# Holding all stores behind the last load, 22 output places and a new instruction order in a fused gated-attention and maxout kernel

## The chip, the cores and the metric

The kernel runs on one core of a Trainium2 chip. The metric is device time in microseconds (us), from launch to end, of that core. The trace's span, from the first to the last traced instruction, is a little shorter. Every number below is from a timed run or from a trace, unless the Trainium skill is named for it. "TensorE" is PE in the profile, "VectorE" DVE, "ScalarE" ACT, "GpSimd" POOL, and "SyncE" SP, the engine that issues nearly all transfers here, in the order of its own instruction stream.

## The reference, cut to what matters

```python
# q, k, v, alpha: (4, 8, 768, 48) float32; out: (3072, 384) float32
for t in range(S):                                  # S = 768
    state = alpha[:, :, t, :, None] * state + einsum('bhd,bhe->bhde', k[:, :, t], v[:, :, t])
    y[:, :, t] = einsum('bhd,bhde->bhe', q[:, :, t], state)
x = y.transpose(0, 2, 1, 3).reshape(B * S, H * D)   # (3072, 384)
g = maximum(x @ w1, x @ w2)                         # w1, w2: (384, 1024)
out = g @ w_out                                     # (1024, 384)
```

Inputs are 4.72 MB each for q, k, v and alpha, weights another 4.72 MB, and 4.72 MB are written.

## The kernel before

The 3072 tokens are cut into 24 chunks of 128. The first six chunks (the first batch) are loaded and computed as three pairs; their tiles carry a d in front (`dcs`, `dqt`, `dpt`, `dy`). The other 18 are single chunks: four loads of 192 KB each, so 72 loads. Per chunk, `loga` is the logarithm of alpha, `cs` its cumulative sum as a matrix product, `ep` and `en` its exponentials, `qt` and `kt` the scaled q and k, `tp` their transposes, `pa`/`pb` the masked scores (`pt`), `T` the carried state, `y` the attention output. Then come the maxout products: `h`, `g`, `op` and the output row block.

The program is ordered while it is built. Each piece of work is an `Op` with its engines, dependencies, buffers and a priority. A list scheduler with a model of durations decides, from a table `PLAN` of nudges, which piece is emitted next on which engine. Each engine then runs its own list strictly in that order, SyncE too. The parts that matter here:

```python
def load(n, i):                     # single chunks: into the old weight staging buffers, six chunks deep
    ...
    nc.sync.dma_start(out=t, in_=src[b, :, c * C : (c + 1) * C, :].rearrange("h p d -> p h d"))

def oevict(e, t0):                  # output rows from PSUM to SBUF; NO = 6 places
    outs[t0] = mo.tile([128, DM], FP32, tag="outs", name="outs", bufs=NO)
    copy(e, outs[t0], ops[t0])

def store(t0):
    nc.sync.dma_start(out=out[t0 : t0 + C, :], in_=outs[t0])
# ... (cut)
op("st", a + i, {"SP": 0.55}, lambda e, t=a0 + i * C: store(t), lat=1.2, deps=[ev], reads=[bs],
   prio=-1, slack=3.0 if a + i < NCG - 4 else 0.0)

def dcs(m, h):                      # cumulative sum of a pair of chunks: 4 wide and 4 narrow products
    l = [loga[:, j, hr(h), 0:D] for j in range(2)]
    nc.tensor.matmul(cs[:, 0:X], lhsT=c11, rhs=l[0], start=True, stop=False)
    nc.tensor.matmul(cs[:, X : 2 * X], lhsT=c11, rhs=l[0], start=False, stop=False)
    nc.tensor.matmul(cs[:, X : 2 * X], lhsT=c11, rhs=l[1], start=False, stop=False)
    nc.tensor.matmul(cs[:, 0:X], lhsT=c01, rhs=l[1], start=False, stop=False)
    # ... four products of 4 columns
```

A store thus stands among the loads. When SyncE reaches one whose output is not ready, the loads behind it wait too.

Of the kernel before, what the change touches and what calls it, by code (L numbers as in the profile page):

```python
# [15 lines left out]
class Op:  # L16


    def __init__(self, sched, name, n, engs, fn, deps=(), lat=0.1, alloc=(), reads=(), prio=0.0, tiled=False, after=(), slack=0.0,
                 shared=False):  # L20
        early, wait, only = PLAN.get(f"{name} {n}", (0.0, 0.0, None))
        engs = {only: engs[only]} if only in engs else engs
        prio, slack = prio + early, slack + wait
        self.name, self.n, self.engs, self.fn, self.lat = name, n, engs, fn, lat
        self.deps, self.alloc, self.prio, self.tiled = [d for d in deps if d is not None], list(alloc), prio, tiled
        self.after = [d for d in after if d is not None]
        self.left, self.done, self.slack, self.shared = None, None, slack, shared
        for b in list(alloc) + list(reads):
            b.users.append(self)
        for e in engs:  # L30
            sched.todo[e].append(self)
# [22 lines left out]
class Banks:  # L54
# [21 lines left out]
COLD = {"m": 2.0, "dp4": 1.3}  # L76
# [4 lines left out]
    "den (2, 1)": (0.0, 0.8, None), "f (0, 4)": (-2.0, 0.0, None), "dm1 (2, 0)": (-1.0, 0.4, None),  # L81
    "dt32 (1, 0)": (0.0, 0.8, None), "m0 21": (0.0, 0.2, None), "v2 15": (0.0, 0.8, None), "qt 19": (-3.7, 0.0, None),
    "oev 12": (0.0, 0.0, 'ACT'), "dv2 (0, 1)": (-1.0, 0.0, None), "w2c (1, 1)": (0.0, 0.4, None),
    "m0 6": (0.0, 0.6, None), "relu (4, 2)": (0.0, 0.4, None), "p3 23": (2.0, 0.0, None), "m 2": (-20.0, 0.0, None),
    "relu (13, 7)": (-4.0, 0.0, None), "ep 18": (20.0, 0.0, None), "mev 2": (4.0, 0.8, None),
    "p2 20": (-900.0, 0.0, None), "mask 0": (21.0, 0.0, None), "den (2, 0)": (-3.0, 0.0, 'DVE'),
    "p3 14": (-900.0, 0.0, None), "T0 19": (0.0, 0.0, 'POOL'), "dp1 (0, 1)": (0.0, 0.2, 'ACT'),
    "dqt (1, 1)": (-0.3, 0.0, None), "w2c (0, 0)": (-0.3, 0.0, 'ACT'), "dm0 (0, 0)": (0.0, 0.8, None),
    "relu (4, 4)": (0.0, 0.4, None), "dp3 (1, 0)": (-1.0, 0.2, None), "f (19, 1)": (900.0, 0.0, None),
    "one 2": (898.0, 0.0, None), "one 0": (-900.0, 0.4, None), "p1 16": (-20.0, 0.0, None),  # L90
    "dep (2, 1)": (0.3, 0.0, None), "en 13": (0.0, 0.8, None), "w 12": (0.0, 0.8, None), "p2 12": (0.0, 0.4, None),
    "dgg (2, 1)": (0.0, 0.4, None), "w 10": (0.0, 0.0, 'DVE'), "dt32 (0, 1)": (-2.3, 0.0, None),
    "t32 14": (0.3, 0.0, 'ACT'), "p2 16": (2.0, 0.0, None), "f (2, 0)": (0.0, 0.2, None),
    "t (5, 1)": (-900.0, 0.2, None), "en 11": (0.0, 0.2, None), "dT1 (0, 1)": (2.0, 0.0, None),
    "dT0 (0, 1)": (1.0, 0.0, None), "f (2, 7)": (-0.3, 0.0, None), "v2 16": (0.0, 0.8, None),
    "dv2 (1, 0)": (0.0, 0.0, 'DVE'), "g 11": (4.0, 0.0, None), "dT0 (1, 0)": (0.0, 0.8, None),
    "relu (7, 0)": (-2.0, 0.0, None), "t (1, 1)": (0.3, 0.0, None), "a1 11": (20.0, 0.4, None),
    "dg (0, 1)": (1.3, 0.0, None), "qt 23": (-899.0, 0.0, None), "oev 6": (0.0, 0.2, None),
    "p3 8": (-900.0, 0.0, None), "T1 7": (6.0, 0.0, None), "one 1": (-1.0, 0.0, None), "f (0, 0)": (-4.0, 0.0, None),
    "dv (1, 0)": (1.0, 0.0, None), "v1 15": (1.0, 0.0, None), "relu (13, 4)": (0.0, 0.0, 'POOL'),  # L100
    "v2 6": (0.0, 0.8, None), "f (13, 0)": (-900.0, 0.0, None), "f (0, 1)": (-2.0, 0.0, None),
    "da3 (0, 0)": (20.3, 0.0, None), "dkt (1, 1)": (0.0, 0.0, 'ACT'), "p2 23": (0.3, 0.0, None),
    "g 17": (0.0, 0.8, None), "dv2 (1, 1)": (0.0, 0.0, 'DVE'), "qt 7": (0.3, 0.0, None),
    "dp1 (2, 1)": (-900.0, 0.0, None), "kt 7": (-0.3, 0.0, None), "dv (2, 1)": (0.0, 0.2, None),
    "m0 11": (900.0, 0.0, None),
# [3 lines left out]
class Sched:  # L109
# [7 lines left out]
    def __init__(self):  # L117
        self.todo = {e: [] for e in ("PE", "ACT", "DVE", "POOL", "SP")}
        self.free = {e: 0.0 for e in self.todo}
        self.wire = 2.0  # L120
        self.tiled = False
        self.refill = None
# [51 lines left out]
    def run(self):  # L174
        while True:
# [14 lines left out]
            if e == "PE" and t < 19.0:  # L190
                cost *= COLD.get(op.name, 1.65)
            if op.shared:

                cost += min(cost, max(0.0, self.free["POOL"] - t) / 2)
            if e == "PE" and op.tiled != self.tiled:
                cost += 0.09
# [21 lines left out]
def kernel(  # L218
# [27 lines left out]
    ND = NCH // 2  # L246
# [8 lines left out]
    ldp = ctx.enter_context(tc.tile_pool(name="ldp", bufs=2))  # L255
# [14 lines left out]
    def load(n, i):  # L270
# [4 lines left out]
        o = (4 * (n % 2) + i) * H * D  # L275
        t = loads[n][i] = flat[:, o : o + H * D].rearrange("p (h d) -> p h d", h=H)
        nc.sync.dma_start(out=t, in_=src[b, :, c * C : (c + 1) * C, :].rearrange("h p d -> p h d"))

    dloads = {m: [None] * 4 for m in range(ND)}

    def dload(m, i, h=None):
        src, tag = SRC[i]
        if dloads[m][i] is None:
            dloads[m][i] = ldp.tile([128, H, 2 * D], FP32, tag="d" + tag, name="d" + tag, bufs=2)
# [3 lines left out]
            in_=src[0, hs, m * C2 : (m + 1) * C2, :].rearrange("h (p j) d -> p h (j d)", j=2),  # L288
# [61 lines left out]
    NB, NQ, NPT = 3, 4, 4  # L350
# [13 lines left out]
    def set_mask():  # L364
        for u in range(2):
            ps = slice(64 * u, 64 * u + 64)
            for jk, jq in ((0, 0), (0, 1), (1, 1)):
                nc.vector.tensor_copy(out=cmask[ps, jk, 64 * jq : 64 * jq + 64], in_=u16[ps, ps])
            nc.vector.tensor_sub(out=cmask[ps, 1, 0:64], in0=u16[ps, ps], in1=ident16[ps, ps])
# [26 lines left out]
    xT = constp.tile([128, 3, NT], FP16)  # L396

# [36 lines left out]
    def v1k(n):  # L434
        nc.gpsimd.tensor_mul(out=kts[n % NB][:, :, 0:D], in0=loads[n][1], in1=st[n]["en"])  # L435

    def v1v(n, t):
        vp = loads[n][3].rearrange("p (r t) d -> p t r d", t=2)
        nc.gpsimd.tensor_copy(out=v16s[n % NB][:, :, 64 * t : 64 * t + D], in_=vp[:, t])
# [5 lines left out]
    def vT(n, t):  # L445
# [4 lines left out]
        nc.gpsimd.tensor_mul(  # L450
# [5 lines left out]
    def vt32(n):  # L456
        t32 = st[n]["t32"] = wk.tile([128, NP, D], FP32, tag="t32", name="t32")
        nc.gpsimd.tensor_mul(  # L458
# [106 lines left out]

    def dcs(m, h):
# [4 lines left out]
        nc.tensor.matmul(cs[:, 0:X], lhsT=c11, rhs=l[0], start=True, stop=False)  # L571
        nc.tensor.matmul(cs[:, X : 2 * X], lhsT=c11, rhs=l[0], start=False, stop=False)
        nc.tensor.matmul(cs[:, X : 2 * X], lhsT=c11, rhs=l[1], start=False, stop=False)
        nc.tensor.matmul(cs[:, 0:X], lhsT=c01, rhs=l[1], start=False, stop=False)
        for r in range(2):
            o = 2 * X + 4 * r
            for j in range(2):
                nc.tensor.matmul(
                    cs[:, o : o + 4], lhsT=loga[:, j, 4 * h + 2 * r : 4 * h + 2 * r + 2, :], rhs=gcol4,
                    start=False, stop=(r == 1 and j == 1),  # L580
                )
# [17 lines left out]
    def dqk(m, h, i):  # L599
# [3 lines left out]
        else:  # L603
            nc.gpsimd.tensor_mul(out=dkts[m % 2][:, :, hr(h), 0:D], in0=src, in1=sd[m]["en"][:, :, hr(h)])  # L604
# [45 lines left out]
    def more(m, u):  # L650
        return u == 0 or m < ND - 1
# [17 lines left out]
    def dw(m, u):  # L669
# [3 lines left out]
        if m == 0 and u == 0:  # L673
# [12 lines left out]
    def dt32(m, u):  # L686
        m1, u1 = dbefore(m, u)
        t32 = sd[m]["t32", u] = wk.tile([128, NP, D], FP32, tag="dt32", name="dt32")
        nc.gpsimd.tensor_mul(out=t32, in0=sd[m1]["w", u1], in1=sd[m]["g", u].unsqueeze(2).to_broadcast([128, NP, D]))

    def dT(m, u, t):
        m1, u1 = dbefore(m, u)
        ps = slice(64 * t, 64 * t + D)
        nc.gpsimd.tensor_mul(
# [4 lines left out]
    def dy(m):  # L699
# [13 lines left out]
        for u in range(2):  # L713
            if u == 1 or m:
# [93 lines left out]
    def ocols(e, t0, c):  # L808
        if c == 0:
            outs[t0] = mo.tile([128, DM], FP32, tag="outs", name="outs", bufs=NO)  # L810
# [7 lines left out]
    outs = {}  # L818

    def oevict(e, t0):  # L820
        outs[t0] = mo.tile([128, DM], FP32, tag="outs", name="outs", bufs=NO)
# [6 lines left out]
    NG, NO = 3, 6  # L828
# [5 lines left out]
    rg16, ro = Ring(NG), Ring(NO)  # L834
# [9 lines left out]
    LOAD, WLOAD = 1.0, 4.12  # L844
# [14 lines left out]
    def dloads_of(m, margin):  # L859
        nonlocal prev  # L860
        dbl.append([Buf(r) for r in rdl])
        parts = [(i, h) for h in (0, 1) for i in (0, 1, 2)] + [(3, None)] if m == 0 else [(i, None) for i in range(4)]
        for i, h in parts:
            prev = op("dld", m, {"SP": DL[m] / (1 if h is None else 2)}, lambda e, i=i, h=h: dload(m, i, h), lat=margin,
                      alloc=[dbl[m][i]] if not h else (), reads=[dbl[m][i]] if h else (), after=[prev], prio=0.3 + m)
# [6 lines left out]
    for x in "d0 w20 w21 wo0 wo1 w10 w11 d1 d2".split():  # L872
        if x[0] == "d":
            dloads_of(int(x[1]), (1.0, 1.9, 1.8)[int(x[1])])
        else:
# [10 lines left out]
           for f in range(0, NF, 2)]  # L886
    for n in range(2 * ND, NCG):
# [28 lines left out]
    smask = op("mask", 0, {"DVE": 1.8}, lambda e: set_mask(), prio=0.1)  # L916
# [7 lines left out]
    for m in range(ND):  # L924
# [18 lines left out]
        for h in range(2):  # L943
# [3 lines left out]
                alloc=al("loga"), reads=[L[0]] + re("loga"))  # L947
            add("p1", h, {"PE": 0.43}, lambda e, m=m, h=h: dcs(m, h), [g["a1", h]], lat=0.17, alloc=[("cs", h)], reads=["loga"])
# [6 lines left out]
            add("kt", h, {"POOL": 0.94}, lambda e, m=m, h=h: dqk(m, h, 1), [g["en", h], g["ld", 1, h]],  # L955
                alloc=al("kt"), reads=["en", L[1]] + re("kt"))
            add("qt", h, {"DVE": 0.47}, lambda e, m=m, h=h: dqk(m, h, 2), [g["ep", h], g["ld", 2, h]], shared=True,
                alloc=al("qt"), reads=["ep", L[2]] + re("qt"))
# [178 lines left out]
```

## Time and profile before

| | before |
|---|---|
| timed runs supplied with the kernel | 147.58 us median of 3 (147.46 to 147.76) |
| time of the profiled run itself, and its span | 144.87 us, 143.1 us |
| TensorE busy | 128.9 us, 90% of the span |
| DMA share, first four fifths of the span | 0.8 to 1.0 in nearly every slice |

The run that was traced took 144.87 us and its span is 143.1 us. The profile lines for this kernel stand in the prediction below.

### The profile page before, as it was taken

The numbers are of one execution on the slowest core, as the hardware profiler recorded it, in microseconds if no ns is written. First come the engines' busy times: TensorE is split into PE (matmuls) and PEld (weight loads), VectorE is DVE, ScalarE is ACT, GpSimd is POOL, SyncE is SP. The second block draws the span as 40 slices with busy tenths as digits, with TensorE's granted clock in tenths as the row PEclk, the third lists the DMA queues.
The fourth block names the chain that finished last, engine by engine and source line by source line (L and its number), as shares of the span: only waits on it lengthen the run. The fifth ranks groups of instructions, "written<-read, shape, count | busy, mean of one in ns | idle before, by whom it ended". The sixth has DMA issues, their size and how long they took to land.

```text
span 143.1 us, 4890 instructions
## 1 busy us (share of the span) xinstructions
PE 128.9 (90%) x1969; PEld 89.4 (62%) x1969; DVE 88.6 (62%) x167; ACT 96.1 (67%) x221; POOL 81.8 (57%) x183
## 2 busy tenths in 40 slices
PE   0377899996999999999999999987999999999991
PEld 0266647774777666766676666645666676666770
DVE  4639739599698985978586858444767856600100
ACT  3552946836876797669785978559659964674541
POOL 6896300499976967776379498407687953400000
PEclk9999999999999999999999999999999999999999
DMA  4999999999989889999899799979998992000403
GB/s 114 250 332 385 379 364 250 233 268 230 202 184 220 175 167 220 236 183 239 200 241 191 175 235 208 184 156 245 225 239 168 223 235 105 35 30 5 165 0 110
DMA packets 93686, 28.62 MB, mean 200 GB/s; under 512 B 87904, under 2 KB 92128, under 8 KB 93664
## 3 DMA queue, kind: packets, MB, share of 16 engines
q1 hardware_dynamic: 93520, 28.22, 83.0%
q8 instruction: 15, 0.25, 0.7%
q10 hardware_dynamic: 144, 0.10, 0.2%
q14 instruction: 7, 0.06, 0.1%
HBM read 23.59 MB, written 4.72 MB: 198 GB/s over the span
## 4 chain that ended last, share of the span: by engine, by line
PE 70%; POOL 10%; DMA 6%; DVE 5%; SPq 3%; issue 2%; ACT 2%; POOLq 0%; ACTq 0%
PE h L777 17%; PE op L794 17%; PE op L791 6%; PE y L548 5%; PE mp L766 4%; DMA wof<-in_alpha_dram 4%; PE pa L489 3%; PE tp L471 3%; DMA daf<-in_alpha_dram 3%; PE dy L710 3%; PE tp L473 2%; POOL kt L435 2%; PE cs L413 2%; PE dtp L616 2%; POOL dkt L604 2%
## 5 line engine op out<-in xcount | busy, mean ns | idle before, releaser
L794 PE MATMUL op<-wo,g 128*128 128x384 f16 x184 | 35.5, 326 | 0.0
L777 PE MATMUL h<-xT,wd 128*128 128x384 f16 (+1 forms) x216 | 34.2, 308 | 0.0
L777 PEld LDWEIGHTS <-wd 128*128 128x128 f16 x216 | 20.3, 98 | 9.0
L794 PEld LDWEIGHTS <-g 128*128 128x128 f16 x184 | 17.2, 98 | 10.7
L784 ACT ACTIVATE g<-h 128x384 f16<-128x384 f32 (+1 forms) x52 | 22.1, 462 | 1.5 <-PE h L777 1.2
L738 ACT COPY qk<-tp 128x1024 f16<-128x1024 f16 x15 | 15.2, 1014 | 4.3 <-PE tp L473 4.2
L508 DVE TENSOR_TENSOR pt<-pa,u 128x512 f16<-128x512 f32 x18 | 11.9, 687 | 9.7 <-PE pa L489 5.4
L782 DVE TENSOR_SCALAR g<-h 128x384 f16<-128x384 f32 (+1 forms) x20 | 9.9, 514 | 12.8 <-PE h L777 12.6
L450 POOL TENSOR_TENSOR T<-w,g 48x192 f16<-48x192 f32 x30 | 15.1, 502 | 1.2
L738 ACT COPY outs<-op 128x384 f32<-128x384 f32 x18 | 8.8, 488 | 9.8 <-PE op L794 9.8
L791 PE MATMUL op<-m,xT 128*128 128x384 f16 x69 | 15.0, 325 | 0.0
L604 POOL TENSOR_TENSOR dkt<-dkf,den 128x384 f16<-128x384 f32 x6 | 6.5, 1085 | 11.7 <-ACT den L586 11.6
L508 DVE TENSOR_TENSOR pt<-pb,u 128x512 f16<-128x512 f32 x18 | 11.8, 680 | 0.0
L519 DVE TENSOR_TENSOR w<-kv,t 48x192 f32<-48x192 f32 x24 | 8.5, 352 | 2.4 <-POOL t L458 1.3
L552 ACT CAST xT<-y 128x384 f16<-128x384 f32 x18 | 8.0, 478 | 2.9 <-PE y L548 2.8
L423 ACT ACTIVATE en<-cs 128x384 f32<-128x384 f32 x18 | 9.0, 497 | 1.1 <-PE cs L417 1.0
L423 ACT ACTIVATE ep<-cs 128x384 f32<-128x384 f32 x18 | 9.0, 499 | 0.0
L435 POOL TENSOR_TENSOR kt<-wof,en 128x384 f16<-128x384 f32 x6 | 6.3, 1056 | 4.2 <-ACT en L423 4.2
L548 PE MATMUL y<-pt,v 128*32 128x128 f16 x288 | 8.2, 219 | 0.0
L791 PEld LDWEIGHTS <-xT 128*128 128x128 f16 x69 | 6.1, 97 | 3.1
L435 POOL TENSOR_TENSOR kt<-w1f,en 128x384 f16<-128x384 f32 x6 | 6.3, 1055 | 2.4 <-issue 1.4
L435 POOL TENSOR_TENSOR kt<-w2f,en 128x384 f16<-128x384 f32 x6 | 6.3, 1054 | 2.4 <-POOL T L450 1.8
(126 smaller groups left out, 275.4 us busy)
## 6 DMA issues: line engine op xcount, KB each, us to landing
out_dram<-outs SPq DMA_DIRECT2D x23, 192.0 KB, 3.1
w2f<-in_moe_w_dram SPq DMA_DIRECT2D x2, 768.0 KB, 7.7
wof<-in_moe_w_out_dram SPq DMA_DIRECT2D x2, 768.0 KB, 10.5
w1f<-in_moe_w_dram SPq DMA_DIRECT2D x2, 768.0 KB, 12.5
dvf<-in_v_dram SPq DMA_DIRECT2D x3, 384.0 KB, 5.8
wof<-in_alpha_dram SPq DMA_DIRECT2D x6, 192.0 KB, 4.5
wof<-in_k_dram SPq DMA_DIRECT2D x6, 192.0 KB, 4.4
wof<-in_q_dram SPq DMA_DIRECT2D x6, 192.0 KB, 4.1
```

Source lines behind the costliest of these rows:

```text
L423: nc.scalar.activation(out=t, in_=csv, func=ACTF.Exp, scale=scale)
L435: nc.gpsimd.tensor_mul(out=kts[n % NB][:, :, 0:D], in0=loads[n][1], in1=st[n]["en"])
L450: nc.gpsimd.tensor_mul(out=st[n]["T16"][ps, :, D * t : D * t + D], in0=st[n - 1]["w"][ps], in1=st[n]["g"][ps].unsqueeze(2).to_broadcast([D ...
L508: nc.vector.tensor_mul(out=s["pt"][:, t], in0=s["pp"][t], in1=ub)
L548: nc.tensor.matmul(y[o : o + 32, b // 4, :], lhsT=lhsT, rhs=rhs, start=start, stop=stop)
L604: nc.gpsimd.tensor_mul(out=dkts[m % 2][:, :, hr(h), 0:D], in0=src, in1=sd[m]["en"][:, :, hr(h)])
L738: {"ACT": nc.scalar.copy, "DVE": nc.vector.tensor_copy, "POOL": nc.gpsimd.tensor_copy}[e](out=out, in_=in_)
L777: nc.tensor.matmul(h[:, 0:W], lhsT=wd16[:, s, f * 128 : (f + 1) * 128], rhs=xT[:, s, a : a + W], start=(s == 0), stop=(s == 2))
L782: nc.vector.tensor_relu(gts[a][:, f, 0:W], hs[a, f][:, 0:W])
L784: nc.scalar.activation(out=gts[a][:, f, 0:W], in_=hs[a, f][:, 0:W], func=ACTF.Relu)
L791: nc.tensor.matmul(op, lhsT=xT[:, s, t0 : t0 + C], rhs=m16[:, s, :], start=(s == 0), stop=False)
L794: nc.tensor.matmul(op, lhsT=gts[a][:, f, i * C : (i + 1) * C], rhs=wo16[:, f, :], start=False, stop=(f == NF - 1))
```

## The change

The intent is to give TensorE its inputs sooner. All stores go behind the last load in SyncE's list, so outputs have to be kept in SBUF: in 22 places, 16 of which are halves of the first batch's load buffers. These load buffers (`dl`) become fixed tiles, where they were tiles of a pool. With them comes a new build-time order. Cut to its core:

```diff
-            op("st", a + i, ..., prio=-1, slack=3.0 if a + i < NCG - 4 else 0.0)
+            op("st", a + i, ..., prio=-1, after=[G[NCG - 1]["ld", 3]])

+    dl = [[constp.tile([128, H, 2 * D], FP32, name=f"dl{j}{i}") for i in range(4)] for j in range(2)]
+    rooms = [constp.tile([128, DM], FP32, name=f"out{i}") for i in range(NO)]          # NO = 6
+    for j in (1, 0):
+        for i in range(4):
+            flat = dl[j][i].rearrange("p h d -> p (h d)")
+            rooms += [flat[:, 0:DM], flat[:, DM : 2 * DM]]
     def oevict(e, t0):
-        outs[t0] = mo.tile([128, DM], FP32, tag="outs", name="outs", bufs=NO)
+        room(t0)                                     # rooms in turn

+    def dsum(e, m, h):                               # VectorE adds the two logarithms of a pair
+        EW[e].tensor_add(out=l[:, 1, hr(h), 0:D], in0=l[:, 1, hr(h), 0:D], in1=l[:, 0, hr(h), 0:D])
     def dcs(m, h):                                   # 3 wide and 2 narrow products
-        nc.tensor.matmul(cs[:, 0:X], lhsT=c11, rhs=l[0], start=True, stop=False)
-        nc.tensor.matmul(cs[:, X : 2 * X], lhsT=c11, rhs=l[0], start=False, stop=False)
-        nc.tensor.matmul(cs[:, X : 2 * X], lhsT=c11, rhs=l[1], start=False, stop=False)
+        nc.tensor.matmul(cs[:, X : 2 * X], lhsT=c11, rhs=l[1], start=True, stop=False)
         nc.tensor.matmul(cs[:, 0:X], lhsT=c01, rhs=l[1], start=False, stop=False)
+        nc.tensor.matmul(cs[:, 0:X], lhsT=ident16, rhs=l[0], start=False, stop=False)

-            add("kt", h, {"POOL": 0.94}, ...)        # the same for v, t32, T, in pairs and single chunks
+            add("kt", h, {"POOL": 0.94, "DVE": 0.47}, ...)
+class PE: ...                                        # a finer model of TensorE in the scheduler
-PLAN = {...}                                         # another table of nudges
+PLAN = {...}
# ... (cut: the mask made in two halves, start values of the model, places of the loads in the staging buffers)
```

## The prediction

> **What bounds the kernel now.** I read the page first (busy shares, slices), then busy time by stretch, then what TensorE waited for, the chain of waits around its late gap, and SyncE's order of issue.
>
> ```profile
> PE 128.9 (90%) x1969; PEld 89.4 (62%) x1969; DVE 88.6 (62%) x167; ACT 96.1 (67%) x221; POOL 81.8 (57%) x183
> ...
> PE   0377899996999999999999999987999999999991
> ...
> DMA  4999999999989889999899799979998992000403
> ```
>
> TensorE (PE) is busy 90% of the 143.1 us span. Its low slices are the first five, the tenth (32 to 36 us), the 27th and 28th (93 to 100 us) and the last. The DMA row is full too, up to the 33rd slice (118 us): a second near-bound.
>
> ```profile
> 42.00:54.00 12.00, 12.00 (x212) 8.00 (x211) 10.41 (x20) 9.12 (x22) 8.82 (x19) 1.00 0.97 191
> ...
> 86.00:97.00 11.00, 9.94 (x139) 6.53 (x137) 6.32 (x12) 6.98 (x17) 5.34 (x13) 1.00 0.89 184
> ...
> 116.00:123.00 7.00, 7.00 (x134) 4.87 (x131) 4.65 (x8) 4.59 (x10) 4.25 (x10) 1.00 0.40 120
> ```
>
> Columns: stretch, length, busy us of PE, PEld, DVE, ACT, POOL, clock, DMA share, GB/s. In 42 to 54, when SyncE issues no store, the loads alone fill the queues (0.97) at only 191 GB/s: one load of 192 KB (196,608 bytes) takes 1.03 us. PE is full beside it. From 86 to 97 PE loses 1.06 us. After 116 the loads are over.
>
> ```profile
> PE dcs L571 <- ACT dloga L561: 6.1, 2, 4.1
> PE dpa L633 <- DVE dqk L738: 1.6, 2, 0.8
> PE cs L413 <- ACT loga L408: 1.4, 1, 1.4
> PE dy L710 <- POOL dT L694: 1.3, 1, 1.3
> ```
>
> These four waits are nearly all of PE's idle time before the end (total, times, longest). The first two are the start, when data arrives. After 20 us only two remain: 1.3 us at 33.8 (POOL writes the state tile dT late) and 1.4 us at 95.9. The chain explains the latter:
>
> ```profile
> 89.13 0.74 SPq L277
> 89.92 0.75 SPq L277
> 90.76 0.70 SPq L277
> 91.51 5.14 DMA wof<-in_alpha_dram
> 96.73 0.53 ACT loga L408
> 97.31 0.32 PE cs L413
> ```
>
> An alpha load issued at 91.51 lands 5.14 us later, ACT takes its logarithm, and PE starts. The load came late because SyncE issued 15 stores among the 72 single-chunk loads between 29.9 and 115.1 us. That stretch has a DMA share of 0.98, 83.5 us of full queues. The 72 loads need 72 x 1.03 = 74.2 us of it, which leaves 9.3 us, or 0.6 us a store. Per chunk of 128 tokens the queues need 85.2/18 = 4.73 us with stores, against PE's 4.66 us a chunk (mean step between the cs products of the chunks from 37.2 to 116.5 us). Loads lose their lead slowly until PE meets the edge once.
>
> **What the Trainium skill says.** "DMA: Bandwidth & Descriptors", Specifications: line rate needs transfers of at least 512 B. The trace agrees: 87,904 of 93,686 packets are under 512 B, and these loads reach 191 GB/s, while the slice carrying weights shows 385. "TensorE: Matmul & The Clock Gate", the section on 56 ns against 53.3 ns: matmuls start N/1.2 GHz apart cold, N/2.4 GHz plus about 2.5 ns warm. Agreed: the products mp (N=384) start 0.314 us apart at 18.1 us and 0.162 us at the end of their group, and 12 h products late in the run take 1.95 us. So PE's work is a sum of column counts, and only idle gaps and cold time can be won. "SBUF — State Buffer", Two separate sides: the port pair that VectorE and GpSimd share is an exclusive lock, taken by a VectorE operation with two SBUF inputs against a GpSimd operation that reads SBUF. Agreed: dqt took 1.08 us beside POOL's dkt (5.90 us), 0.55 us beside a POOL memset (9.36 us).
>
> **The change, part by part.**
>
> 1. *Stores behind all loads.* In the built order of SyncE all 90 loads stand first, then all stores (the last half row stays on ACT's queue). The queues need 4 x 1.03 = 4.12 us a chunk against PE's 4.66. The single loads start near 29.9 us, so the last is issued near 29.9 + 74.2 = 104 us instead of 113.5, unless a ring slot (six chunks deep) delays it. The 95.9 gap goes: minus 1.37 us. This is all that the 9 us of DMA time is worth, because PE is dense on both sides of the gap. The held stores cost 24 x 0.6 = 14 us of queue time after 104, ending near 119, well before the last output (140 us); the end keeps its 3.0 us from the last product to the last landing.
> 2. *22 output places.* Six own and 16 halves of the first batch's load buffers, idle after some 38 us. Some 15 outputs are made before the loads end, so none should wait for a place.
> 3. *A shorter cumulative sum for the first batch.* VectorE adds the two logarithms, and dcs falls from 4 wide and 4 narrow products to 3 and 2: 18 products fewer in all (1951 for 1969, by the built order). A warm dcs took 0.435 us (two in 25.89 to 26.76); without one wide (0.08) and two narrow (0.02 to 0.03 each) it is 0.30. Four warm ones: minus 0.5 us of PE, but they now wait for an addition on VectorE (0.15 to 0.35 us) in a stretch ruled by arrivals, so I count minus 0.25.
> 4. *New order; some POOL work may go to DVE or ACT.* It should mend the dT wait (up to minus 1.3). I worked the first 38 us by hand, with durations and landing times of the trace and the new order. Up to 24.8 us nothing can be won: w1 lands at 20.9 and 22.96, four wd subtractions on DVE take 0.92 us each, and h needs them all. The sums for the second pair of chunks stand behind these on DVE, until 25.7, so dcs (after 15 h products) waits some 0.6 us. Then the m=1 part comes earlier (kt on DVE and POOL together), but its four masks on DVE follow dqk and the next sums and end near 35.0, so dy ends near 36.1; before it ended at 36.0. One idle time replaces another: minus 0.2, with 0.7 either way.
> 5. *Switches.* Small tiled products stand in 22 groups instead of 20. A group costs some 0.2 us of unfilled time (0.09 before y at 90.55, 0.12 after pa at 91.7), but three changes inside groups (0.1 each) go: plus 0.1.
> 6. *New small gaps* of a fresh order: plus 0.1.
>
> Sum: -1.37 - 0.25 - 0.2 + 0.1 + 0.1 = -1.6 us. Span 141.5, and with the 4.5 us by which the median time exceeds the span (147.58 - 143.1), 146.0. Orders of this kind are usually chosen by trial on a chip, which my hand working cannot see; for that I move 0.3 us down, a choice: **145.7 us**.
>
> **The rivals.**
>
> - *All idle goes.* From 25.89 to 140.06 us PE has 114.2 us with 2.8 idle: 111.4 of work, from which part 3 takes 0.5. Without any gap the span would be some 143.1 - 2.8 - 0.5 = 139.8, time 144.3, minus 2.2%. For it: POOL, the engine of the early wait, is relieved. Against it: weights and the chain of one pair of chunks bind up to 36 us. So over 2% needs nearly everything.
> - *Loads were no bound: the transfer is hidden anyway.* Then only order counts, and the time stays at 147 to 147.5. For it: PE is full in nearly every stretch, and one gap of 1.4 us is little. Against it: the chain names the DMA.
> - *DVE becomes the bound.* It takes most of the moved POOL work, and waits in order behind weight casts (its half of w2 lands at 12.1 us, and the second dqt stands behind it). If the first output stage slips by 2 us, the time is 148 to 149. For it: DVE is already 10.41 of 12 us busy in 42 to 54. Against it: elsewhere it has a third of its time free, and the same work took POOL longer.
> - *Stores pile up at the end.* 14 us of queue time fit before the end; a store still queued at 139 would cost up to 1 us. Little speaks for it.
>
> **Range and chances.** The gap at 95.9 is nearly sure (1.4 us). The first 38 us are uncertain by about 0.9, new gaps by 0.7: together some 1.1 us. A range of 8 in 10 is 144.3 (the floor of the first rival) to 147.1. Over 2% faster means below 144.63, so 0.2; over 2% slower is above 150.5, 0.03; the rest is 0.77.
>
> **What would show it.** Right: no PE wait on loga after 40 us; SyncE's last load near 104 to 106 us and stores in one block behind it; DMA share full to 108 or so and some 350 GB/s or more right after; PE 10.0 of 10 us in every stretch from 40 to 130; dy of the second pair ending near 36. Wrong: dy ending before 35 (the order won more, time under 144.6); a PE wait on a load even without stores (loads are bound by slots or latency); PE waits on DVE tiles above 1 us in the middle; stores landing at the very end behind others.

## The result, and the profile after

| | before | after |
|---|---|---|
| same rounds, one chip | 147.52 us median of 4 (145.65 to 147.76) | 142.21 us median of 4 (141.91 to 142.58) |
| profiled run: time, span | 144.87, 143.1 | 142.58, 140.7 |

A ratio is the mean time of one kernel's fast runs over that of the other's in the same rounds, so it is not quite the ratio of the medians quoted beside it. Here it is 0.9668, with a 95% interval of 0.9586 to 0.975. The kernel became 3.3% faster. For a kernel on one core, a run is "slow" when it is over 1.5% above the fastest of the same kernel, so leaving slow runs out cuts the upper end of a kernel that spreads: on the second chip below it takes 6 of 11 runs of before, and there the medians (147.59 and 142.25) differ by 5.3 us, the means of fast runs by 4.2. The prediction said 145.7 us with a range of 144.3 to 147.1, "within 2%" as the likeliest: its direction was right, its size and its range were wrong.

These lines of the page of the kernel after answer to those shown of before (busy time; then PE and DMA in 40 slices):

```profile
PE 126.3 (90%) x1951; PEld 87.4 (62%) x1951; DVE 105.0 (75%) x218; ACT 97.8 (69%) x233; POOL 58.5 (42%) x126
...
PE   0147999799799999999999999999999999999991
...
DMA  4999999999899899989999799999979988012013
```

TensorE's row has no low digit after the eleventh slice. Work has moved from GpSimd (81.8 to 58.5 us) to VectorE (88.6 to 105.0), which is still far from full. Busy time by stretch of the kernel after, with the columns as in the prediction:

```profile
42.00:54.00 12.00, 12.00 (x244) 8.60 (x240) 10.46 (x24) 9.90 (x27) 6.40 (x11) 1.00 0.97 190
86.00:97.00 11.00, 11.00 (x168) 7.44 (x157) 9.69 (x20) 9.97 (x23) 4.08 (x8) 1.00 1.01 197
110.00:118.00 8.00, 8.00 (x128) 5.39 (x125) 6.84 (x15) 6.40 (x17) 3.10 (x6) 1.00 0.96 344
118.00:125.00 7.00, 7.00 (x87) 4.47 (x86) 4.83 (x9) 4.20 (x9) 1.00 (x3) 1.00 0.15 55
```

From 86 to 97 us, where TensorE lost 1.06 us before, it is now full. From 110 to 118 the DMA moves 344 GB/s: these are the stores, with rows of 1536 bytes. From 118 the queues are all but empty, though TensorE works until 137.7. What TensorE waited for after (total, times, longest), all of it:

```profile
PE dcs L610 <- DVE dloga L602: 7.0, 2, 6.5
PE dtp L653 <- DVE dqt L639: 2.9, 3, 1.6
PE dpa L670 <- ACT dqk L775: 0.6, 1, 0.6
PE wtp L789 <- DVE w L775: 0.2, 1, 0.2
```

No wait on `loga` is left, and none on `dT`. SyncE's issue order at the end of the loads (start, length, then what):

```profile
105.66 1.32 SPq L302 DMA_DIRECT2D w1f<-in_v_dram  x1
107.04 3.50 SPq L870 DMA_DIRECT2D out_dram<-out  x6
110.58 15.86 SPq L870 DMA_DIRECT2D out_dram<-dl  x14
```

The last load is issued at 105.66 us, and then the stores follow in one block.

**Where the time went.** I cut each trace at one common point: the start of the `cs` product of the eighth chunk ("cs7"), near 41 us. Behind it, both orders hold the same work, so the stretch from cs7 to the end of TensorE's work (read at the start of its last product) compares the middle and the end, and cs7 itself the front.

| trace | span | cs7 starts | cs7 to TensorE's end |
|---|---|---|---|
| before, supplied profile | 143.1 | 42.12 | 97.78 |
| before, two further looks | 144.6, 143.8 | 41.13, 41.97 | 100.28, 98.68 |
| after, three traces | 140.7, 140.3, 139.7 | 41.63, 41.21, 40.68 | 95.88, 95.88, 95.88 |

The means differ by 3.6 us of span (143.83 against 140.23): 3.0 of it behind cs7 (98.91 against 95.88), and 0.6 in front of it (41.74 against 41.17). The experiments ask what makes up each, and why the timed medians differ by more, 5.3 us.

### The profile page after: what moved, and what is told of

Same layout as the page of the kernel before. It is cut to its first block, busy times and chain, and to the rows that moved or that the text cites. A ratio compares the mean times of both kernels' runs of the same rounds, so it can differ in the third digit from the quotient of the medians.

```text
span 140.7 us, 4883 instructions
## 1 busy us (share of the span) xinstructions
PE 126.3 (90%) x1951; PEld 87.4 (62%) x1951; DVE 105.0 (75%) x218; ACT 97.8 (69%) x233; POOL 58.5 (42%) x126
## 4 chain that ended last, share of the span: by engine, by line
PE 75%; DMA 8%; SPq 8%; ACT 2%; DVE 2%; POOL 2%; issue 1%; POOLq 0%
PE op L831 21%; PE h L814 21%; DMA dl<-in_alpha_dram 8%; PE op L828 8%; PE y L581 6%; SPq L338 4%; PE pa L522 4%; PE tp L504 3%; PE tp L506 3%; SPq L318 3%; PE cs L446 2%; PE kv L533 2%; DVE dpt L681 1%; PE cs L450 1%; PE opc L842 1%; POOL dkt L641 1%
## 5 line engine op out<-in xcount | busy, mean ns | idle before, releaser
L831 PE MATMUL op<-wo,g 128*128 128x384 f16 x184 | 36.0, 326 | 0.0
L814 PE MATMUL h<-xT,wd 128*128 128x384 f16 (+1 forms) x216 | 35.2, 308 | 0.0
L814 PEld LDWEIGHTS <-wd 128*128 128x128 f16 x216 | 19.8, 98 | 8.5
L775 ACT COPY qk<-tp 128x1024 f16<-128x1024 f16 x14 | 14.2, 1013 | 3.1 <-PE tp L506 2.9
L775 ACT COPY dl<-op 128x384 f32<-128x384 f32 x15 | 7.3, 485 | 9.3 <-PE op L831 9.3
L476 POOL TENSOR_TENSOR g<-gg 128x4 f32<-128x4 f32 x15 | 7.3, 488 | 7.6 <-ACT gg L460 5.5
L483 POOL TENSOR_TENSOR T<-w,g 48x192 f16<-48x192 f32 x15 | 9.2, 613 | 1.0
L468 POOL TENSOR_TENSOR kt<-wof,en 128x384 f16<-128x384 f32 x5 | 5.3, 1062 | 10.1 <-ACT en L456 10.0
L468 POOL TENSOR_TENSOR kt<-w1f,en 128x384 f16<-128x384 f32 x5 | 5.0, 998 | 8.7 <-ACT en L456 8.6
L641 POOL TENSOR_TENSOR dkt<-dl,den 128x384 f16<-128x384 f32 x3 | 3.3, 1106 | 12.6 <-ACT den L623 11.6
```

Of the source, the lines that this page charges most:

```text
L468: EW[e].tensor_mul(out=kts[n % NB][:, :, 0:D], in0=loads[n][1], in1=st[n]["en"])
L483: EW[e].tensor_mul(out=st[n]["T16"][ps, :, D * t : D * t + D], in0=st[n - 1]["w"][ps], in1=st[n]["g"][ps].unsqueeze(2).to_broadcast([D, NP ...
L775: {"ACT": nc.scalar.copy, "DVE": nc.vector.tensor_copy, "POOL": nc.gpsimd.tensor_copy}[e](out=out, in_=in_)
L814: nc.tensor.matmul(h[:, 0:W], lhsT=wd16[:, s, f * 128 : (f + 1) * 128], rhs=xT[:, s, a : a + W], start=(s == 0), stop=(s == 2))
L831: nc.tensor.matmul(op, lhsT=gts[a][:, f, i * C : (i + 1) * C], rhs=wo16[:, f, :], start=False, stop=(f == NF - 1))
```

## The experiments

The kernels were run in four groups, each on a chip of its own, and those of one group share the runs of the kernel before. The first held `before_again`, `e1`, `e2` and `e3`; the second `after_again`, `e1b`, `e3b` and `e5`; the third the two looks, `e6` and `e7`; the fourth `e8`, `e9`, `e2b` and `after_third`. A "b" is the same kernel again.

The theory: SyncE's stores, mixed among the loads, push the loads so late that TensorE waits, more often in most runs than in the one that was traced; holding them back wins this, and the new order wins something at the front. The first rival: the order and the engine choices win nearly all, and the stores only look guilty. The second rival, for the stores themselves: not the queue time of the writes costs, but that SyncE, in order, stands at a store whose output is not ready. All sixteen kernels run for this gave correct results.

### The kernel before again

No edit.

> The kernel before, unchanged, to see why its usual time (147.5 us) is 2.7 us above the one profiled run (144.87 us, span 143.1). Theory A (the queues, with stores among the loads, sit at the edge, and the late-load gap of TensorE grows in the usual run): several runs near 147.5 with a span near 145.7, and in their trace TensorE waits on loga (loads) for 3 to 5 us in total instead of 1.4. Rival B (the start varies: TensorE's clock or the landing of the first loads): the extra 2.6 us lies before 40 us and the wait on loads stays near 1.4. Rival C (a fixed cost outside the span): spans stay at 143.1 while the times are 147.5.

Measured: 145.15 us mean of its fast runs against 145.37 of the kernel before in the same rounds (ratio 0.9989), medians 145.67 and 145.76. So in these rounds the kernel before is 1.8 us quicker than where the change was measured (147.52). Its traced run was a slow one (146.6 us, span 144.8, granted clock 0.988), so I compare no time with it, but it shows something that the clock row of the first profile did not. TensorE by stretch (length, PE, PEld, DVE, ACT, POOL, clock, DMA share, GB/s):

```profile
30.00:36.00 6.00, 4.62 (x184) 3.51 (x181) 6.00 (x11) 3.44 (x10) 5.69 (x11) 1.00 1.18 231
...
36.00:38.00 2.00, 1.86 (x31) 1.48 (x30) 0.91 (x2) 1.34 (x3) 2.00 (x5) 0.59 0.87 205
38.00:39.00 1.00, 1.00 (x30) 0.77 (x27) 0.18 (x1) 1.00 (x3) 0.82 (x3) 0.50 1.01 205
```

After six microseconds in which TensorE was busy for 4.62, its clock fell to half for some 3 us. The next chunk's step (cs6 to cs7) took 5.59 us instead of 4.91. What makes it fall is not shown: in the supplied trace TensorE was busy for 4.61 of the same six, in the first look below for 4.48, and both kept a clock of 1.00. Such a run's mean clock is 0.976 to 0.988. That was so in 24 of 66 runs of the old order (the kernel before and its two variants with held stores), and in none of 40 of the new order (after, and its variants with mixed stores or the old sum). Most runs of the kernel before have no such dip. The 19 of its runs that have one took 146.0 us in the mean and the 30 without it 146.0 too, slow runs counted, so the dip does not explain the spread.

### The old order, with the stores held

TensorE's, VectorE's, ScalarE's and GpSimd's lists stay as before; only SyncE's changes, and the 22 places are added, and with them the fixed load buffers `dl` into which the first batch is loaded.

```diff
-            op.fn(e)
+            if op.name == "st" and self.loads < 72:
+                self.held.append((op, e))
+            else:
+                op.fn(e)
+            self.loads += op.name == "ld"
+            if op.name == "ld" and self.loads == 72:
+                for o, x in self.held:
+                    o.fn(x)
# ... (cut: the 22 places and the load buffers dl, as in the change)
```

> The old order on TensorE, ACT, DVE and POOL, instruction for instruction; only SyncE's list is changed: all stores stand behind the last load, with 22 output places as in the change. Theory A (stores among loads are most of the loss): 142.5 to 143.5 us, ratio 0.970, narrow spread, no TensorE wait on loga after 40 us. Rival B (the new order is most of the gain): 146 to 147 us, ratio 0.995.

Measured: 142.86 us against 145.37 (ratio 0.9832, 0.9777 to 0.9887), median 142.84. From cs7 to the end its trace takes 95.98 us, as little as after the whole change. What TensorE waited for:

```profile
PE dcs L579 <- ACT dloga L569: 5.9, 2, 3.9
PE dpa L641 <- DVE dqk L746: 1.6, 2, 0.8
PE dy L718 <- POOL dT L702: 1.3, 1, 1.3
```

The waits for `loga` are gone, those of the front are all there. So holding the stores, with the places and load buffers that go with it, gives the whole gain behind cs7, without any new order, and with GpSimd doing all that it did. The second time, on another chip:

> The old order with held stores again, for a comparison on one chip. 142.5 to 143.0 us; against the kernel before minus 2.5 to minus 3 us.

Measured: 142.42 us against 146.46 (ratio 0.9695), median 142.78. Its traced run was a slow one and no time is compared with it. Holding the stores was worth 2.5 us on the first chip and 4.0 on this one, more than the 2.5 to 3 expected. The variant itself agrees within 0.5 us on both; it is the kernel before that moved.

### The new order, with the stores mixed in

The four compute engines' lists stay as after. A store goes back among the loads, 3 us of model time after its output, which is the rule of before.

```diff
+            if op.name == "ld":
+                while self.pend and self.pend[0].ready <= t:
+                    self.pend.pop(0).fn("SP")
+            if op.name == "oev" and op.st is not None:
+                op.st.ready = op.done + 3.0
+                self.pend.append(op.st)
```

> The new order on the four compute engines, instruction for instruction, with each store put back among the loads (3 us after its output is made in the scheduler's order, as the kernel before did it), still 22 places. Theory A: 145 to 147 us, TensorE waits 2 to 5 us on loads somewhere between 60 and 115 us. Rival B: 142 to 143.5 us, as the changed kernel.

Measured: 143.26 us against 145.37 (ratio 0.9859), median 143.12. The waits for `loga` are back:

```profile
PE cs L457 <- ACT loga L452: 1.2, 3, 0.8
```

From cs7 to the end it takes 98.24 us, 2.4 more than with the stores held. On a fourth chip, together with the kernel after:

> The new order with stores among the loads again, now on one chip with the changed kernel: 1 to 1.5 us above it (143.2 to 143.7), if holding the stores is worth less in the new order than the 2.5 to 4 us it was in the old one.

Measured: 142.16 us against 144.44 (ratio 0.9847), median 142.28.

> The changed kernel on the same chip, for the difference from e2b: 142.0 to 142.4 us.

Measured: 142.23 us, ratio 0.9847, median 142.16. On this chip holding the stores was worth nothing in the new order, and the mixed trace takes 95.88 us from cs7, as the kernel after does. So the two parts overlap. Either alone gives 2.1 to 4.0 us, both together 4.2 (second chip) and 2.2 (fourth). Whether late loads are felt at all differs from run to run: the mixed kernel felt them on the first chip and not on the fourth.

### The old sum, in the new order

The addition on VectorE is taken out and `dcs` has its 4 wide and 4 narrow products again. All else is as after.

```diff
     def dsum(e, m, h):
-        EW[e].tensor_add(...)
     def dcs(m, h):
+        # the four wide and four narrow products of before
```

> The changed kernel with the old cumulative sum of the first batch (4 wide and 4 narrow products, no addition on DVE), same order otherwise. If the shorter sum is worth what its products take (4 warm ones of 0.13 us and two cold ones), it is 0.5 us slower than the changed kernel: 142.7. If the wait for the addition costs as much as it saves: 142.2, no difference. In the trace the first dcs should start near 4.1 instead of 6.5 us.

Measured: 141.82 us against 145.37 (ratio 0.9766), median 141.53. On the second chip, beside the kernel after:

> The changed kernel with the old cumulative sum again. If the shorter sum costs more (its addition waits behind the masks and pads on DVE: first dcs at 6.5 instead of 4.0 us) than its 18 fewer products save, this is 0.3 to 0.7 us faster than after_again. If the start is hidden by the weights' landing, it is 0.3 to 0.5 us slower or level.

Measured: 141.46 us against 146.46 (ratio 0.963), median 141.49.

> The changed kernel, unchanged, on one chip with the old order with held stores (e1b) and with its old-sum variant (e3b). Theory: with stores held in both, the new order is worth what the front shows: 1.0 to 1.2 us against e1b (about 141.7 here if e1b is 142.8). Rival: it is worth nothing (142.8), and the profiled run that showed it level with e1 at 40 us was the usual case.

Measured: 142.21 us against 146.46 (ratio 0.9682), median 142.25. With stores held in both, the new order as it stands is thus worth 0.2 us against `e1b` (142.42), not the 1.0 to 1.2 of the theory; with the old sum it is worth 1.0 (141.46, and on the first chip 141.82 against 142.86). The shorter sum, which spares 18 products, costs 0.75 us. The first wait of TensorE with the old sum:

```profile
PE dcs L608 <- ACT dloga L594: 4.0, 1, 4.0
```

The first sum starts at 3.98 us, when the logarithm is there. After the change the same wait ends at 6.52 us, and its releaser is VectorE, which has to clear pads and write masks before it gets to the addition. From cs7 to the end nothing changes (95.90), and cs7 itself starts at 40.43 instead of a mean of 41.17, so all of the gain lies at the front. This variant is the fastest: it beats the kernel before and the kernel after.

### The front's work back on GpSimd

In the new order, the pair work that had moved to VectorE or ScalarE is emitted on GpSimd at the same place.

```diff
-            op.fn(e)
+            back = op.name in ("dkt", "dT0", "dT1", "dt32") or (op.name == "dv" and op.n[0] > 0)
+            op.fn("POOL" if back else e)
```

> The changed kernel's order of issue, with the first batch's dkt, dT, dt32 and dv (but for the very first dv) put back on POOL, the rest as changed. If moving this work off POOL made the front's gain of the new order, TensorE waits on POOL tiles before 38 us for 1 to 3 us more and the time is 1 to 3 us above after_again (142.7 to 145). If not, it is within 0.5 us of it.

Measured: 143.98 us against 146.46 (ratio 0.9802), median 143.89, which is 1.8 us more than the kernel after in the same rounds. New waits of TensorE:

```profile
PE dkv L699 <- POOL dv L776: 1.2, 3, 0.7
PE dkv L699 <- POOL dkt L642: 0.6, 1, 0.6
```

That they also sum to 1.8 us is chance: other waits shrank, and this traced run (143.18 us, the quickest of its six) reaches cs7 at 41.88 us, only 0.7 later than `after_again` (41.21). From cs7 on it takes 95.88 us like the kernel after. Relief of GpSimd therefore matters in the first 40 us. It doesn't behind: in the old order with held stores GpSimd kept everything, and TensorE had no wait after 40 us. The test is not a clean removal, as the order was chosen for the other assignment.

### Two looks at the kernel before

No edit; these were taken because the supplied profile showed one late load while the medians said more.

> A second look at a profile of the kernel before, since the first profiled run (144.87 us) was quicker than its usual one. Theory: whatever the time, the span is the time less 1.8 to 2.0 us, and what a slower run has more lies between 60 and 115 us, as late loads of single chunks: 0.2 to 1 us at several chunks besides the one of 1.4 us.

Measured: 146.36 us, span 144.6, clock 1.0, one run. Its span is 1.5 us longer than that of the first profile although cs6 starts 1.0 us earlier (36.25 against 37.21). The views: waits of TensorE; three links of the chain around the last late load; and the stretch of the loss.

```profile
PE dcs L571 <- ACT dloga L561: 5.9, 2, 4.1
PE cs L413 <- ACT loga L408: 1.7, 3, 1.1
...
PE tp L473 <- POOL kt L435: 0.7, 1, 0.7
```

```profile
86.58 5.02 DMA w1f<-in_v_dram
...
92.50 4.75 DMA wof<-in_alpha_dram
...
97.91 0.32 PE cs L413
```

```profile
86.00:97.00 11.00, 10.64 (x152) 6.91 (x149) 7.01 (x14) 7.01 (x16) 5.17 (x14) 1.00 0.88 183
```

TensorE meets late data three times, not once, and not only late alpha: the chain also runs through a v load of 5.02 us. The step between `cs` products is some 0.3 to 0.7 us longer than in the supplied trace at five places from the tenth chunk on. The DMA share in this stretch is 0.88, though loads are late: the queues are not full.

> The same once more, for the spread: between two runs of different length the start of each chunk's cs product differs in steps at late loads, and not evenly. Rival: the difference is all there before 40 us (landing of the weights, clock).

Measured: 145.61 us, span 143.8, clock 0.997, one run; 98.68 us from cs7, waits on `loga` 1.4 us.

### Every store twice

To double the suspected cost, each store was written twice to the same rows.

```diff
     def store(t0):
         nc.sync.dma_start(out=out[t0 : t0 + C, :], in_=outs[t0])
+        nc.sync.dma_start(out=out[t0 : t0 + C, :], in_=outs[t0])
```

> The kernel before with each full store issued twice (the same rows again), all else the same: 15 more stores of 0.6 us among the loads, 9 us more for the queues. Theory A (the queues are at the edge there): nearly all of it shows, 7 to 10 us more than before (154 to 157 if before is 147). Rival (the queues had room, the order of issue mattered): 0 to 2 us more.

Measured: 183.14 us against 146.03 (ratio 1.2525), median 183.56.

> The changed kernel with each full store issued twice behind the loads: 46 instead of 23, some 28 us of queue time after the last load at about 105 us, so done near 133, still ahead of the last output at 138. Theory A: 142 to 143 us, at most 1 us more than the changed kernel (the last doubled store). Rival (held stores collide with the end): 2 us more or worse.

Measured: 169.68 us against 146.03 (ratio 1.1591), median 169.74. Both are misses as tests. The edit brought a wait of its own, seen in what SyncE waited for in the second:

```profile
SPq L871 <- DMA out_dram<-dl: 24.7, 16, 1.9
SPq L871 <- DMA out_dram<-out: 11.2, 7, 2.1
```

The second store to the same rows waits on SyncE until the first has landed, 35.9 us in 23 times, 1.6 us each, and one pair takes some 2.4 us in all. "DMA: Bandwidth & Descriptors", in "Anatomy of one DMA — SWDGE (gpsimd) path", of the Trainium skill says that most of a transfer's fixed cost of about 2 us is the confirmation that the last byte has landed; that page describes the other issuing path, and these runs show a wait of like size. The pairs measure this latency, not the queue time of a store. They show at least that a SyncE that waits in order between loads is ruinous: the old order lost 37 us.

### Extra reads in the places of the stores

A read that nobody uses takes queue time but waits for no output. Fifteen reads of 192 KB with 1536-byte rows were put in front of the first fifteen stores of the kernel before, and, in the other kernel, at the same places in the old order with the stores held.

```diff
+    def extra_read():                       # the first 15 times
+        nc.sync.dma_start(out=scratch[left[0] % 5], in_=moe_w_out[0:128, :])
     def store(t0):
+        extra_read()                        # e8; in e9 called where a store is held back
```

> The kernel before with an unused read of 192 KB (rows of 1536 B, into scratch) issued just before each of its 15 stores among the loads; unlike the doubled stores it waits for no landing. Theory A (queue time at the edge): an extra read takes 0.5 to 0.6 us of queue time, 8 to 9 us in all, and 4 to 9 us of it show in the time. Rival (what delays loads is SyncE waiting in order for the outputs of its stores): 0 to 1 us more.

Measured: 154.50 us against 144.44 (ratio 1.0696), median 154.71. That is 10.1 us more, a little above the 4 to 9 of theory A. From cs7 to the end its trace takes 106.85 us, and TensorE's waits for `loga` are:

```profile
PE cs L420 <- ACT loga L415: 6.8, 7, 1.9
```

> The old order with held stores (e1), with the same 15 unused reads where the stores had stood. They take queue time but wait for no output. Theory A: the loss comes back nearly whole, 2.5 to 4 us above e1 (level with the kernel before, within 1 us). Rival (SyncE's waits in order for outputs): no loss, 142.4 to 143.

Measured: 142.73 us against 144.44 (ratio 0.9882), median 143.04. From cs7 to the end it takes 95.98 us, just as without the reads. The stretch in which before lost most:

```profile
86.00:97.00 11.00, 11.00 (x155) 7.43 (x153) 6.75 (x14) 8.89 (x22) 5.77 (x13) 1.00 0.97 195
```

The reads delay the loads: the alpha load of the last chunk is issued at 107.43 us instead of 100.26, so 7.2 us for 15 reads, 0.48 us each, and TensorE notices none of it. The same view over the traces shows a knee:

| trace | issue of the last chunk's alpha load | cs7 to TensorE's end | over 95.9 |
|---|---|---|---|
| old order, stores held | 100.26 | 95.98 | 0.1 |
| after, three traces | 100.57, 101.68, 104.80 | 95.88 | 0.0 |
| old order, held, 15 reads | 107.43 | 95.98 | 0.1 |
| new order, mixed, fourth chip | 108.42 | 95.88 | 0.0 |
| before, supplied profile | 109.98 | 97.78 | 1.9 |
| before, second look | 110.91 | 98.68 | 2.8 |
| before, first look | 111.53 | 100.28 | 4.4 |
| new order, mixed, first chip | 111.56 | 98.24 | 2.3 |
| before with 15 reads more | 119.66 | 106.85 | 10.9 |

Up to an issue at some 108 us, delay is free in these traces. At 110 a loss is there, and between 108.4 and 119.7 it averages 0.97 us per us. The kernel before sits 1.6 to 3.1 us behind the last free point, so a difference of 1 us between two runs or chips can turn into time directly, and the changed kernel sits 3.6 to 7.9 us in front of it. That this is why the one spreads (by 2.9 to 3.7 us among the eleven runs of three groups) more than the other (0.9 and 1.9 us among six) is argued and not shown: the old order with held stores spreads by 1.6, 2.7 and 3.4 us among six, slow runs counted.

Did SyncE stand at stores whose output was not ready? The kept traces say no. In the first look, one output is written to SBUF, and its store and the next two are issued, at:

```profile
76.78 0.56 DVE L738 COPY outs<-op 128x384 f32<-128x384 f32 x1 [0.45 <-PE op L794]
```

```profile
85.37 0.65 SPq L825 DMA_DIRECT2D out_dram<-outs  x1
...
98.55 1.11 SPq L825 DMA_DIRECT2D out_dram<-outs  x2
```

The store comes 8.0 us after its output. With outputs and stores taken in order, each of the fifteen stores among the loads comes 5.9 to 9.1 us after its output in the three traces of before that aren't marked slow, and 3.2 us or more in the two mixed ones. The low share of 0.88 was no sign of such a stand either, as no store is issued from 86.1 to 98.5 us. So the second rival fails, although the time of `e9` came out as it said: there the reads stayed in front of the knee.

What delays the loads is queue time, but not that of the stores alone. The last alpha load of before is 9.7 to 11.3 us later than with held stores (109.98 to 111.53 against 100.26). Of this, 1.1 to 1.6 us are there before any store: the first single load is issued at 29.41 to 29.91 us in before, and at 28.31 in `e1`. In the stretch in front of it (before, then `e1`) the queues are equally full:

```profile
22.00:29.00 7.00, 7.00 (x63) 5.33 (x62) 5.22 (x8) 5.64 (x17) 1.88 (x2) 1.00 1.03 242
```

```profile
22.00:29.00 7.00, 7.00 (x64) 5.31 (x62) 5.09 (x8) 6.22 (x19) 2.44 (x3) 1.00 1.03 272
```

All six traces with the old load buffers move 239 to 248 GB/s here, all twelve with the new ones 249 to 282. So the new load buffers are a rival for a part of the gain; why they help is not shown, and no run puts them alone into the kernel before. By the slope of the knee they may be worth up to some 1.6 us, an estimate. The rest, 8.1 to 10.2 us, is 0.54 to 0.68 us for each store, about its queue time: at 344 GB/s its 196,608 bytes take 0.57 us. The extra reads, counted in the same way, cost 0.50 us each. With equal buffers, mixed stores cost 2.4 us behind cs7 in one trace and nothing in the other.

## Why the prediction was right or wrong

**Right in mechanism.** The four signs that it named for the stores all came: no wait on `loga` after 40 us, the last load at 105.66 us (said: 104 to 106; 104.50 and 107.42 in the other two traces), the stores in one block with 344 GB/s right behind it (said: some 350), TensorE full in every stretch from 40 to 130 us. The 22 places cost no wait (part 2), VectorE at 75% did not become the bound, no store was left for the end, and neither switches nor new gaps (parts 5 and 6, 0.1 each) are seen from cs7 on.

**Wrong: the conversion from span to time.** The step "with the 4.5 us by which the median time exceeds the span (147.58 - 143.1), 146.0" failed. In 126 runs that list both, time less span is 1.7 to 2.1 us, in both kernels and the variants; the profiled run of before gives 144.87 - 143.1 = 1.8. The other 2.7 us were not overhead but the distance from this quick execution to an ordinary one. With 1.85 us the predicted span of 141.5 gives 143.4, or 143.1 with the 0.3 moved by choice, instead of 145.7. This step alone put the range out of reach.

**Wrong: part 1, mis-sized.** "The 95.9 gap goes: minus 1.37 us. This is all that the 9 us of DMA time is worth" was read off one wait of one trace. In that trace the stretch behind cs7 was 1.8 us longer than with the stores held, and over three traces 3.0 us. The prediction had found the near-balance of the queues (4.73 us a chunk) and TensorE (4.66), and should have concluded that the loss varies with the run. The two failures are linked: part of what the 4.5 us held was late loading, and a change that removes late loading removes it too.

**Wrong: part 4, mis-sized.** "One idle time replaces another: minus 0.2, with 0.7 either way" is too little. With the old sum the new order reaches cs7 at 40.43 us, and before reached it at 41.74 in the mean of three traces: 1.3 us earlier. By my list, masks "end near 35.0, so dy ends near 36.1". They ended at 34.46, and `dy` at 34.95, against 36.0 before, which is the first of the prediction's own signs of being wrong ("dy ending before 35"); the wait for `dT` went and none came in its place. The run with the front's work back on GpSimd, 1.8 us slower, shows that the moved work is needed for it, in this order. The wait of 0.6 us for the sums was right (0.52). One thing that I had not looked for is TensorE's speed earlier on. The first `mp` products, in TensorE's timeline after and before (start, length, form, count):

```profile
17.28 1.47 PE L803 MATMUL mp<-wo,w2T 128*128 128x384 f16 x8
```

```profile
18.13 2.71 PE L766 MATMUL mp<-wo,w2T 128*128 128x384 f16 x8
```

Eight equal products took 1.47 us after the change and 2.71 before, so in this pair of traces they ran at full speed some 3 us earlier; in `after_again` they took 2.22. The profile's clock column shows 1.00 in all three, so only these lengths tell of it. That gain is mostly lost again at the arrival of w1, as the prediction said: `h` began at 22.56 us against 22.3 to 23.3 before.

**Wrong in sign: part 3.** "I count minus 0.25" came out as plus 0.75, since the variant with the old sum is that much faster on the same chip. I had charged the addition at its own length of 0.15 to 0.35 us; what it costs is its place in VectorE's list, which held the first sum back from 3.98 to 6.52 us. Together parts 3 and 4 were put at -0.45 and came to -0.6 at cs7, nearly right by two errors that cancel.

**The sum.** Parts 1 to 6 were given as -1.6 us of span. The traces show -3.6: -3.0 behind cs7, where 1.37 was expected, and -0.6 in front of it. The timed difference on the first measurement is 5.3 us. Its missing 1.7 us belong to runs of before that are slower than any that I have a trace of, slow ones left out (147.5 against 144.9 to 146.4). That those too are late loads fits the knee, but no trace of such a run shows it. Against it stands the one trace of a slow run with held stores (`e1b`, 144.72 us): it reaches cs7 only at 43.55 us and takes 95.98 from there, so a run can also lose its time at the front. Half-clock runs are no explanation, as before is not slower with them. What the 1.7 us are stays open. Of the rivals, "all idle goes" came nearest: its span of 139.8 is close to the 139.7 to 140.7 measured, and its time of 144.3 carries the same 4.5 us. The other three did not happen.

## What to carry to other kernels

Compare the time of the profiled run itself with the ordinary median before taking the profile as typical: where two near-bounds balance to one per cent, one trace shows one sample of a loss that varies. Transfers that nobody waits for don't belong among those somebody does, if the outputs find room; measure the slack by delaying the loads with harmless reads. When a variant brings new buffers along, look for what differs before the first changed instruction. A shortcut that saves one engine's work can cost more through the place in another engine's queue that it needs.

## What the Trainium skill lacked or had wrong

- "Runtime: NRT & Kernel Launch", section "The ~15µs preamble/postamble breakdown", gives a gap of about 6.2 us between a profile's total time and the reported execution time. Here the device time is longer than the trace's span by 1.7 to 2.1 us in 126 runs. The two pairs may not be the same quantities; for this metric the measured figure holds.
- "TensorE: Matmul & The Clock Gate", section "What's actually happening", has the half clock come after at least one idle window of about 3.4 us. In the second trace of before the clock fell to 0.50 at 38 us though TensorE had been busy for 4.62 of the 6 us from 30 to 36 and its longest single wait there was 1.3 us; 24 of 66 runs of the old order had a mean clock of 0.976 to 0.988. The supplied trace, with 4.61 of the same 6 us, kept 1.00, so a busy share does not decide it either.
- "DMA: Bandwidth & Descriptors", Specifications, has the threshold of 512 bytes, and the page gives no measured rate of this chip for rows of 192 bytes: loads in rows of 192 bytes ran at 190 GB/s, stores in rows of 1536 bytes at up to 344 (mean over 8 us). What one transfer of 192 KB among such loads delays them is not there either: 0.5 us for a read, 0.54 to 0.68 for a store.
- No page says that two stores to the same rows, issued one after the other in a program built in this way, are put in sequence by a wait at the issuing engine: 1.6 us of waiting for each of 23 pairs.
- No page warns that a kernel at the edge of two bounds has no single time: the kernel before had medians of 145.2 to 147.6 us in five measurements, the changed one 142.2 on each of the three that it ran on.
